# Two score tiles in one two-bank tile with one exponential, during the second MLP product of a fused attention and token-mixer kernel

## The chip, the cores and the metric

The kernel runs on one core of a Trainium2 chip. The metric is the device time of one execution in microseconds (us). A kernel is timed in several runs, and one more execution is recorded by the hardware profiler; all shares and durations below are from that one. The engines are TensorE (PE, with its weight loads as PEld), VectorE (DVE), ScalarE (ACT), GpSimd (POOL) and SyncE (SP), which issues the DMAs. Matmuls write PSUM, which has eight banks of 512 f32 columns; ACT and DVE read it from there.

## The reference

```
g = sigmoid((x * gate_w).sum(-1, keepdims=True))
# attention: 2048 tokens, 32 query heads of 20, one shared key/value head
q = (x @ wq) by head;  k = x @ wk;  v = x @ wv
p = softmax(q k^T * 20 ** -0.5)
a = (p v, heads side by side) @ wo
# token mixer: the MLP runs along the token axis, 2048 -> 1728 -> 2048, for 640 channels
u = gelu(layernorm(x)^T @ w1 + b1)
b = (u @ w2 + b2)^T
out = g * a + (1 - g) * b
```

All is f32. The MLP uses `A_x` as its input, as the attention does.

## The kernel before

**Units and stretches.** Attention is cut into 512 units: a block of 512 queries, a group of four heads (32 such pairs, `NU`), and one of 16 blocks of 128 keys. A unit has four *score* matmuls (`s`, line 684; 62 rows of the array, 512 columns), each followed by one exponential on ACT (line 695) from the PSUM bank into an SBUF buffer `p`, 128x512. A *max* matmul (`m`, line 515) computes scores the other way round, and a DVE reduction (line 521) takes their row maxima, which the scores of the next head group need. The last step of a unit is the product of its four `p` buffers with `v` (line 798), called PV here.

The middle of the program is a row of 244 *stretches* (`main`, line 1188). A stretch holds the score and max matmuls for two units and a share of the MLP or output projection, the `F` matmuls of 320 columns; it ends with PV of two units, 16 matmuls. In stretches 0 to 83 the F matmuls are the rest of the first MLP product, in 84 to 211 the second MLP product (`b2_jobs`, line 865), in 212 to 243 the output projection. Every matmul of a stretch but PV uses half the array's rows, so two *lanes* run side by side: one has the F matmuls, the other most of the scores and maxima; the halves swap from stretch to stretch.

**The order.** `ORDER` (line 1149) is a table of strings, one for each number of F matmuls in a stretch: `F` is an F matmul, `s` and `m` a score and a max on the other lane, `S` and `M` the same on the F lane. The second MLP product has stretches of 20 F (96 of them) and of 21 F (32). PE runs its instructions in program order, so a matmul that waits holds back all behind it, on both lanes.

**Banks.** `g_bank` holds the F matmuls' accumulator. The other seven banks are seven separate one-bank tiles: three named `ms`, three named `s`, one named `o`. They lie in one list (`pool`), with the time at which a small planner expects each to be free (`after`, `bank_give`); `bank_take` gives the one that is free first, to a score, a max or PV alike, so that a name says nothing of what a bank holds. The semaphore waits are not written by hand: the framework adds them, from the tiles that each instruction writes and reads.

**p buffers.** `next_p` (line 661) asks a pool of `NP` = 12 buffers for the next one.

**Tail.** The last 24 units run in blocks (`BLOCKS`) with larger groups; a block issues the scores up to one or two ahead of what its PV needs.

Of the kernel before, what the change touches and what calls it, by code (L numbers as in the profile page):

```python
# [45 lines left out]
def mix_kernel(ctx: ExitStack, tc: tile.TileContext, A_x, A_wq, A_wk, A_wv, A_wo,  # L46
# [417 lines left out]
    u0 = upool.tile([P, 2 * FC * HD2], F32R, name="u0")  # L464
    u_hi = [view(t, 0, FC) for t in (u0, slot[0])]
    u_lo = [view(t, FC * HD2, FC) for t in (u0, slot[0])]
    pp_pool = ctx.enter_context(tc.tile_pool(name="pp", bufs=NP))
    ev = ctx.enter_context(tc.tile_pool(name="ev", bufs=1))
    mpool = ctx.enter_context(tc.tile_pool(name="mpool", bufs=2))
    mmpool = ctx.enter_context(tc.tile_pool(name="mmpool", bufs=2))  # L470
# [184 lines left out]
    ptiles = {}  # L655
    spare = [False]
    sc = [0, 0]
    ring = [None] * NP
    ready = {}

    def next_p():
        ring.append(ring.pop(0))
        return pp_pool.tile([P, NB], F32, name="p") if ring[-1] is None else ring[-1]

    def s_next(b):
        j = sc[b]
# [10 lines left out]
    def qk(u, pr, b):  # L677
        n, kb = units[u]
        assert n in back_in
        if kb == 4 and pr == 0 and b == 0:  # L680
            new_q(n + 1)
        q = qtiles[n]
        s = lead_bank() if ps_l else bank_take()
        nc.tensor.matmul(s, kst[64 * b:64 * b + 62, kb * P:(kb + 1) * P], q[64 * b:64 * b + 62, pr, :],  # L684
                         start=True, stop=True)
        ready[u] = 0.0 if ps_l else max(ready.get(u, 0.0), bank_give(s, "exp"))
        if not ps_l and len(ptiles) >= len(ring):
            late.append(pool.pop()[1])
        p = next_p()
        ptiles[u, 2 * pr + b] = p  # L690

        behind, last["ins"] = last["ins"], None

        def exp():
            e = nc.scalar.activation(p, s, AF.Exp, scale=SCALE)  # L695
            if behind is not None:
                tc.add_manual_dep(e.ins, behind.ins.name, SYNC, reason="row tiles that share a bank")
                last["sig"] = e

        exp()  # L700

    ps_g = ctx.enter_context(tc.tile_pool(name="ps_g", bufs=1, space=PSUM, side="right"))
    ps_s = ctx.enter_context(tc.tile_pool(name="ps_s", bufs=3, space=PSUM, side="right"))
# [82 lines left out]
    def pv_group(us, keep=False):  # L786
        n, kb = units[us[0]]
        assert units[us[-1]][0] == n
        while late:
            pool.append((max(clock["now"], clock["act"]) + 2 * PV_US, late.pop()))  # L790
        if not otile:
            otile.append(bank_take())
        o = otile[0]
        opened = not keep or kb == 0 or us[0] == len(units) - TAIL
        ends = kb + len(us) == NS
        for i, u in enumerate(us):
            for hh in range(4):
                nc.tensor.matmul(o[32 * hh:32 * hh + 32, :], v_sb[:, kb + i, :], ptiles.pop((u, hh)),  # L798
                                 start=opened and i == 0, stop=(i == len(us) - 1) and (ends or not keep),
                                 skip_group_check=True)  # L800
        if not keep:
            begin = max(clock["act"], clock["pv"] + 0.336)
            clock["act"] = begin + 0.477
            pool.append((begin + 0.657, otile.pop()))
            if kb == 0:
                sums[0] = ev.tile([P, NB], F32, name="acc", bufs=2)
                nc.scalar.activation(sums[0], o, AF.Copy)
            else:
                part = ev.tile([P, NB], F32, name="part", bufs=2)
                nc.scalar.activation(part, o, AF.Copy)  # L810
                nc.gpsimd.tensor_add(sums[0], sums[0], part)  # L811
        if ends and n < NU - 1:
            qb, g = divmod(n, NQ)
# [48 lines left out]
            first = (None, turned, back) if keep else (sums_out, sums_in, None, inverse, inverse_in, None, scale)  # L862
            later.extend((False, f) for f in (*first, high, low))
# [273 lines left out]
    def settle(wide=False):  # L1137
# [6 lines left out]
        for f in q_parts_due[:2]:  # L1144
# [4 lines left out]
    AHEAD, ENTER, EXIT = 4, 0.108, 0.135  # L1149
    ORDER = {26: "mFFsFmFsFFsFFmFmFsFFFsFmFFmFFsFFmFFmFFmFsMFs",  # L1150
             22: "sFmFFsFFFmsFFFmFssFFmFFFssFFFmmFFFsFmM",
             20: "MsmFFsFsFsFFFFmFFsmFmFFFFmsFsFFsFFMm",
             21: "MsFsFFmmFFsFFssFFFmsFFmFFFsmFFmFFsFFm",
             15: "sMFmFsFFmFsFFsFmFFsFFmFsFFsS",
             16: "sMFmFsFFmFsFFsFmFFsFFmFsFFsSm"}

    def order(k):
        return ORDER[len(ph[k][0]) + (k - (len(ph) - 4 * NA) in SIXES)]
# [29 lines left out]
    def main(k, vs, n_max):  # L1188
# [2 lines left out]
        fs, done = list(fs), list(done)  # L1191
        known, kept = set(row_max), set(sent)
        end = 2 * ((vs[-1] if vs else -1) + 1)
        tokens = fit(order(k), "s", end + AHEAD - sc[b])
        tokens = fit(fit(tokens, "m", n_max[b]), "M", n_max[1 - b])
        tokens = "S" * (end - sc[1 - b]) + tokens
        for i, c in enumerate(tokens):
            if i == (len(tokens) + 1) // 2:
                settle()
            if c == "F":  # L1200
                gate = max(clock["sig"], clock["g"]) if len(fs) == len(ph[k][0]) else 0.0
                issue(1 - b, F_US, fs.pop(0), gate)
                clock["behind"] = clock["end"]
                while done and not fs:
                    done.pop(0)()
            else:
                h = b if c in "sm" else 1 - b
                step = (s_next if c in "sS" else ms_next)(h)
                if step:
                    issue(h, X_US, step, min(e for e, _ in pool))  # L1210
# [20 lines left out]

    ps_l.clear()
    in_lead.close()
    ps_m = ctx.enter_context(tc.tile_pool(name="ps_m", bufs=3, space=PSUM))
    ps_o = ctx.enter_context(tc.tile_pool(name="ps_o", bufs=1, space=PSUM))
    tiles = [ps_m.tile([P, NB], F32, name="ms") for _ in range(3)] + s_banks
    tiles.append(ps_o.tile([P, NB], F32, name="o"))
    pool.extend(zip(FREE_AT, tiles))
    v = 0
    clock.update(now=0.0, act=ACT_AT, dve=0.5, pv=0.0)  # L1240
# [22 lines left out]
        tail_load(NS - 4 - NA + i, late=True)  # L1263

    for j, n in enumerate(BLOCKS):
        ends = [min(2 * len(units), 2 * (v + n) + (2 if n < 3 else 1)) for _ in range(2)]
        lanes = [[], []]
        own = [(2 * len(units) - c + 32 * NU - m) * X_US for c, m in zip(sc, given)]
        while any(sc[b] < ends[b] for b in range(2)):
# [46 lines left out]
    ot = ev.tile([P, NB // 32, 32], F32, name="ot")  # L1316
    rl = ev.tile([P, NB // 32], F32, name="rl")
    on = ev.tile([P, NB], F32, name="acc", bufs=2)
    oh, ol = (pp_pool.tile([P, NB], F32, name="p").bitcast(F32R) for _ in range(2))
    half = slice(NB // 2, NB)  # L1320

    def turn(a):
# [29 lines left out]

    def close(i, d):
        st = NS - 4 + i
        at = pp_pool.tile([P, NB], F32, name="p")
# [49 lines left out]
```

## Time and profile before

| | |
|---|---|
| median of the runs, us | 1600.85 (1600.8 to 1601.18, 3 runs) |
| the profiled execution, us | 1600.86 |
| its span, first to last instruction, us | 1599.1 |
| DVE busy | 1355.6 us, 85% |
| ACT busy | 1286.0 us, 80% |
| POOL busy | 868.5 us, 54% |
| PEld busy | 1124.6 us, 70% |

A page of the profile lists the busy time of each engine, the span in 40 slices, the DMA queues, the chain of work that ended last, and the costliest groups of instructions. A row such as `L521 DVE TENSOR_REDUCE mp<-s` is line 521 of the kernel, the engine, the operation, and what it writes and reads. Matmuls overlap each other, so "busy" on PE says that some matmul was under way, not that the array was full. What follows the bar of a group is the idle time of its engine just before it and the instruction that ended the wait.

### The profile page before, as it was taken

How to read it: one execution, taken by the hardware profiler on the slowest of the kernel's cores; microseconds unless marked ns; L12 is line 12 of the kernel's file. 1: busy time of each engine (PE TensorE's matmuls, PEld its weight loads, DVE VectorE, ACT ScalarE, POOL GpSimd, SP SyncE). 2: the span in 40 equal slices, each digit the busy share in tenths (PEclk: the TensorE clock that was granted, in tenths of full speed). 3: DMA queues.
4: the chain of work that ended last, by engine and by line, in shares of the span. 5: the costliest groups of instructions: out<-in, count | busy, mean ns of one | idle time of the engine just before them, and what ended most of it. 6: DMA issues, size and time to landing. Idle time of an engine off the chain costs nothing.

```text
span 1599.1 us, 39478 instructions
## 1 busy us (share of the span) xinstructions
PE 1593.2 (100%) x14864; PEld 1124.6 (70%) x14864; DVE 1355.6 (85%) x2301; ACT 1286.0 (80%) x2566; POOL 868.5 (54%) x976
## 2 busy tenths in 40 slices
PE   9999999999999999999999999999999999999999
PEld 7899677776777667666666666666666666666676
DVE  6689999999999999988888888888888888766643
ACT  4546888888888888888888888888888888999975
POOL 6568677678778777544544344454544433344420
PEclk9999999999999999999999999999999999999999
DMA  7655223223323222222222121222222112345521
GB/s 219 213 168 147 74 66 87 75 69 95 91 79 84 80 74 73 65 73 82 74 69 67 54 68 54 82 73 82 73 74 66 59 50 67 92 122 182 169 78 59
DMA packets 183750, 145.07 MB, mean 91 GB/s; under 512 B 38291, under 2 KB 145424, under 8 KB 183560
## 3 DMA queue, kind: packets, MB, share of 16 engines
q1 hardware_dynamic: 183272, 142.23, 30.7%
q8 instruction: 117, 1.92, 0.5%
q14 instruction: 73, 0.60, 0.1%
q10 hardware_dynamic: 288, 0.33, 0.1%
HBM read 108.75 MB, written 32.15 MB: 88 GB/s over the span
## 4 chain that ended last, share of the span: by engine, by line
PE 98%; DVE 1%; issue 0%; POOL 0%; ACT 0%; DVEq 0%; POOLq 0%
PE s L798 14%; PE ms L798 12%; PE g L876 11%; PE ms L515 9%; PE s L515 8%; PE s L684 8%; PE g L1079 8%; PE ms L684 7%; PE pp L308 4%; PE o L798 4%; PE o L515 3%; PE o L684 3%; PE s L729 2%; PE g L1015 2%; PE s L970 1%; DVE mp L545 1%
## 5 line engine op out<-in xcount | busy, mean ns | idle before, releaser
L521 DVE TENSOR_REDUCE mp<-ms 128x1 f32<-128x512 f32 x909 | 596.8, 682 | 63.2 <-PE ms L515 32.6
L521 DVE TENSOR_REDUCE mp<-s 128x1 f32<-128x512 f32 x785 | 518.8, 682 | 69.6 <-PE s L515 38.4
L695 ACT ACTIVATE p<-s 128x512 f32<-128x512 f32 x915 | 535.4, 631 | 12.1 <-PE s L684 5.2
L695 ACT ACTIVATE p<-ms 128x512 f32<-128x512 f32 x796 | 473.3, 631 | 6.7 <-PE ms L684 2.8
L811 POOL TENSOR_TENSOR acc<-acc,part 128x512 f32<-128x512 f32 x213 | 275.4, 1293 | 307.2 <-ACT part L810 303.4
L684 PE MATMUL s<-qst,kst 62*128 62x512 f32 x919 | 351.4, 407 | 0.2 <-DVE yo L978 0.2
L515 PE MATMUL ms<-kst,qmx 60*128 60x512 f32 x909 | 348.8, 406 | 0.0
L684 PE MATMUL ms<-qst,kst 62*128 62x512 f32 x799 | 311.2, 409 | 0.0
L1079 PE MATMUL g<-slot,wh 64*128 64x320 f32 x1344 | 308.6, 309 | 0.0
L515 PE MATMUL s<-kst,qmx 60*128 60x512 f32 x785 | 304.3, 411 | 0.5 <-DVE mp L521 0.5
L135 POOL TENSOR_TENSOR wl<-wr,wh 128x512 fp32r<-128x512 f32 (+1 forms) x176 | 218.2, 1240 | 28.0 <-ACT wh L132 16.3
L798 PE MATMUL s<-p,v_sb 128*32 128x512 f32 x1856 | 223.2, 598 | 0.0
L1079 PEld LDWEIGHTS g<-slot,wh 64*128 64x128 f32 x1344 | 222.3, 184 | 0.0
L1079 PE MATMUL g<-slot,wl 64*128 64x320 f32 x672 | 212.3, 316 | 0.0
L515 PEld LDWEIGHTS ms<-kst,qmx 60*128 60x128 f32 x909 | 165.6, 185 | 58.2 <-ACT p L695 33.5
L798 PE MATMUL ms<-p,v_sb 128*32 128x512 f32 x1688 | 204.8, 598 | 0.0
L521 DVE TENSOR_REDUCE mp<-o 128x1 f32<-128x512 f32 x262 | 178.9, 683 | 30.5 <-PE o L515 17.4
L695 ACT ACTIVATE p<-o 128x512 f32<-128x512 f32 x308 | 194.6, 632 | 3.7 <-PE o L684 3.0
L876 PE MATMUL g<-slot,wh 64*128 64x320 f32 x864 | 195.2, 308 | 0.0
L876 PE MATMUL g<-u,wh 64*128 64x320 f32 x864 | 195.1, 308 | 0.0
L684 PEld LDWEIGHTS s<-qst,kst 62*128 62x128 f32 x919 | 169.1, 185 | 26.1 <-DVE mp L521 11.7
L515 PEld LDWEIGHTS s<-kst,qmx 60*128 60x128 f32 x785 | 142.9, 185 | 61.4 <-ACT p L695 34.6
(271 smaller groups left out, 3140.0 us busy)
## 6 DMA issues: line engine op xcount, KB each, us to landing
wr<-in_B_w_dram SPq DMA_DIRECT2D x136, 256.0 KB
qmx<-q_scr SPq DMA_DIRECT2D x192, 80.0 KB
qst<-q_scr SPq DMA_DIRECT2D x192, 80.0 KB
ot<-l_scr SPq DMA_DIRECT2D x120, 64.0 KB
y_scr<-yo SPq DMA_DIRECT2D x16, 320.0 KB
slot<-o_scr SPq DMA_DIRECT2D x16, 320.0 KB
o_scr<-ot SPq DMA_DIRECT2D x124, 40.0 KB
o_scr<-acc SPq DMA_DIRECT2D x124, 40.0 KB
```

The costliest lines, as they stand in the source:

```text
L135: nc.gpsimd.tensor_sub(wl[:, :nv], wr[:, :nv], f32(wh[:, :nv]))
L308: nc.tensor.matmul(pp, w, t, start=first and n == 0, stop=not more and n == len(steps) - 1)
L515: nc.tensor.matmul(ms, qmax[n][64 * b:64 * b + 60, pr, qt * P:(qt + 1) * P], kst[64 * b:64 * b + 60, kq * NB:(kq + 1) * NB], start=True, s ...
L521: r = nc.vector.tensor_reduce(mtiles[n][:, c, kq:kq + 1], ms, axis=AX.X, op=ALU.max)
L684: nc.tensor.matmul(s, kst[64 * b:64 * b + 62, kb * P:(kb + 1) * P], q[64 * b:64 * b + 62, pr, :], start=True, stop=True)
L695: e = nc.scalar.activation(p, s, AF.Exp, scale=SCALE)
L729: nc.tensor.matmul(pu[r][:, :HD2], w[rows, c, :], h[rows, st, :], start=(st == 0 and k == 0), stop=(st == NS - 1 and k == 2))
L798: nc.tensor.matmul(o[32 * hh:32 * hh + 32, :], v_sb[:, kb + i, :], ptiles.pop((u, hh)), start=opened and i == 0, stop=(i == len(us) - 1) a ...
L811: nc.gpsimd.tensor_add(sums[0], sums[0], part)
L876: other_tile(half, nc.tensor.matmul(hold["p"][:, :HD2], w[r, i, :], u[d][r, fc, :], start=(hold["n"] == 1), stop=(hold["n"] == 6 * FC - 3)))
L1015: other_tile(half, nc.tensor.matmul(hold["p"][:, :HD2], o[r, c, :], w[r, c, d * HD2:(d + 1) * HD2], start=(hold["n"] == 1), stop=(hold["n" ...
L1079: other_tile(half, nc.tensor.matmul(hold["p"][:, :HD2], w[r, st % HS, :], h[d][r, st, :], start=(hold["n"] == 1), stop=(hold["n"] == 6 * NS)))
```

## The change

Four of the seven banks become two tiles `ms` of two banks each. In a stretch with 20 F, two scores of one lane (`a` and `z` in the order) go to the two halves of one such tile, and a single exponential over 1024 columns reads both and writes two `p` buffers. For that, the twelve `p` buffers become slices of one tile. Outside such a pair, the four halves are handed out singly, as the banks were before; the seventh bank named `o` is gone, so the count stays at seven. The orders for 20 and 21 F are new, with the same number of matmuls of each kind. A score that finds no free `p` buffer now gets its exponential after the next PV (`deferred`). In the tail, a block no longer issues scores ahead of its own PV. Two buffers of the closing code come from other tiles.

```diff
-    pp_pool = ctx.enter_context(tc.tile_pool(name="pp", bufs=NP))
+    pp_pool = ctx.enter_context(tc.tile_pool(name="pp", bufs=1))
+    p_all = pp_pool.tile([P, NP, NB], F32, name="p")
...
-    ring = [None] * NP
+    ring = [p_all[:, i, :] for i in range(NP)]
+    p_slot = {id(p): i for i, p in enumerate(ring)}
...
     def next_p():
         ring.append(ring.pop(0))
-        return pp_pool.tile([P, NB], F32, name="p") if ring[-1] is None else ring[-1]
+        return ring[-1]
+
+    def next_pair():
+        two = sorted((next_p(), next_p()), key=lambda p: p_slot[id(p)])
+        lo, hi = (p_slot[id(p)] for p in two)
+        return two, p_all[:, lo:hi + 1:hi - lo, :]
...
+        if len(ptiles) < len(ring):
+            give()
+        else:
             late.append(pool.pop()[1])
...
+            deferred.append(give)
...
+    def pair_hold():
+        at = {id(t): e for e, t in pool}
+        whole = min(bank_pairs, key=lambda p: max(at[id(t)] for t in p[:2]))
...
+        pool[:] = [x for x in pool if x[1] is not whole[0] and x[1] is not whole[1]]
+
+    def pair_half(b):
...
+        nc.tensor.matmul(two["whole"][i], kst[64 * b:64 * b + 62, kb * P:(kb + 1) * P],
+                         qtiles[n][64 * b:64 * b + 62, pr, :], start=True, stop=True)
...
+        if pr:
...
+            pool.extend((free, two["whole"][i]) for i in two["banks"])
...
+            ps, whole = next_pair()
+            for pr, i in enumerate(two["banks"]):
+                ptiles[u, 2 * pr + b] = ps[i]
+            exp(whole, two["whole"][2], two["behind"])
...
-             20: "MsmFFsFsFsFFFFmFFsmFmFFFFmsFsFFsFFMm",
-             21: "MsFsFFmmFFsFFssFFFmsFFmFFFsmFFmFFsFFm",
+             20: "MsFsFmFFazFFmFFFsFmFFFsFmFFmFFsFsFmM",
+             21: "sFmFsFFmFFFsFFsFmsFFmFmFFFsmFFmFFsFsM",
...
-    ps_m = ctx.enter_context(tc.tile_pool(name="ps_m", bufs=3, space=PSUM))
-    ps_o = ctx.enter_context(tc.tile_pool(name="ps_o", bufs=1, space=PSUM))
-    tiles = [ps_m.tile([P, NB], F32, name="ms") for _ in range(3)] + s_banks
-    tiles.append(ps_o.tile([P, NB], F32, name="o"))
+    ps_m = ctx.enter_context(tc.tile_pool(name="ps_m", bufs=2, space=PSUM))
+    wholes = [ps_m.tile([P, 2, NB], F32, name="ms") for _ in range(2)]
+    bank_pairs = [(t[:, 0, :], t[:, 1, :], t) for t in wholes]
+    tiles = [t for p in bank_pairs for t in p[:2]]
+    tiles = tiles[:3] + s_banks + tiles[3:]
...
-        ends = [min(2 * len(units), 2 * (v + n) + (2 if n < 3 else 1)) for _ in range(2)]
+        ends = [min(2 * len(units), 2 * (v + n)) for _ in range(2)]
```

Two places of PE's order show what this does to the waits. The names carry the framework's numbers here, so that one tile can be told from another; `x2` counts equal rows that follow each other, and `[waits DVE_49]` says that the instruction waits for a count that DVE raises as its instructions end (`Activation_49` for ACT, `Pool_49` for POOL). The first place is the start of stretch 132, with 20 F matmuls, in which `s`, `ms` and `o` are banks and `g` the F accumulator. Before the change (line 515 is a max, 684 a score, 876 an F):

```order
L515 MATMUL s_1187<-kst_71,qmx_13137 128x512 [waits Activation_49]
L684 MATMUL ms_2333<-qst_13138,kst_71 128x512 [waits Activation_49]
L515 MATMUL s_1186<-kst_71,qmx_13137 128x512 [waits DVE_49]
L876 MATMUL g_1185<-u0_1163,wh_13763 128x320 [waits DVE_49,Activation_49,Pool_49]
L876 MATMUL g_1185<-u0_1163,wh_13763 128x320
L684 MATMUL ms_2331<-qst_13138,kst_71 128x512
L876 MATMUL g_1185<-u0_1163,wl_13764 128x320 [waits Pool_49]
L684 MATMUL ms_2332<-qst_13138,kst_71 128x512
```

Here the first five score and max matmuls go to five tiles. The same place after the change (line 516 is a max, 691 a score, 735 a score of the pair, 930 an F):

```order
L516 MATMUL ms_2325<-kst_71,qmx_12182 128x512 [waits Activation_49]
L691 MATMUL ms_2325<-qst_12122,kst_71 128x512 [waits DVE_49]
L930 MATMUL g_1186<-u0_1163,wh_12680 128x320 [waits Activation_49,Pool_49]
L691 MATMUL s_1188<-qst_12122,kst_71 128x512
L930 MATMUL g_1186<-u0_1163,wh_12680 128x320
L516 MATMUL s_1187<-kst_71,qmx_12182 128x512
L930 MATMUL g_1186<-u0_1163,wl_12681 128x320 [waits Pool_49]
L930 MATMUL g_1186<-u0_1163,wh_12680 128x320
L735 MATMUL ms_2326<-qst_12122,kst_71 128x512 x2
```

The first two rows write the two halves of one tile, `ms_2325`. The score in the second row goes to a half that ACT read last, and yet it waits for DVE: by the counts in the program, for the reduction of the max in the first row, which reads the other half. The framework counts readers of a PSUM tile by the whole tile, not by its banks. The second place is the end of the same stretch, up to PV (line 798 before, 849 after). Before:

```order
L684 MATMUL s_1188<-qst_13138,kst_71 128x512 [waits Activation_49]
L876 MATMUL g_1185<-u0_1163,wh_13769 128x320
L876 MATMUL g_1185<-u0_1163,wh_13941 128x320 [waits Pool_49]
L515 MATMUL ms_2333<-kst_71,qmx_13137 128x512 [waits DVE_49]
L515 MATMUL s_1187<-kst_71,qmx_13137 128x512 [waits Activation_49]
L798 MATMUL ms_2331<-p_13969,v_sb_72 32x512 [waits DVE_49]
```

The four tiles of these rows were each last written at least sixteen rows further up. After:

```order
L691 MATMUL ms_2326<-qst_12122,kst_71 128x512
L930 MATMUL g_1186<-u0_1163,wh_12686 128x320
L691 MATMUL ms_2326<-qst_12122,kst_71 128x512 [waits Activation_49]
L930 MATMUL g_1186<-u0_1163,wh_12841 128x320 [waits Pool_49]
L516 MATMUL ms_2325<-kst_71,qmx_12182 128x512 [waits DVE_49] x2
L849 MATMUL s_1188<-p_1167,v_sb_72 32x512 x8
```

The third row waits for the exponential of the score in the first row, two rows ahead. Of the two maxima in the fifth row, the second waits for the reduction of the first. From stretch 0 on, 1821 matmuls into an `ms` tile wait for a reader of the other half that comes later in the program than the last reader of their own half: 717 in stretches 1 to 83, 849 in 84 to 211, 210 in 212 to 243, 38 in the tail and 7 ahead of stretch 1.

More of the change, by code (lines that the diff above doesn't have):

```diff
@@ L686, in qk @@
         ready[u] = 0.0 if ps_l else max(ready.get(u, 0.0), bank_give(s, "exp"))
-        if not ps_l and len(ptiles) >= len(ring):
-            late.append(pool.pop()[1])
[L689 to L697, printed above, removed]
-                last["sig"] = e
@@ L700, in qk, with give, exp @@
-        exp()
+        behind, last["ins"] = last["ins"], None
+        def give():
+            assert len(ptiles) < len(ring)
+            p = ptiles[u, 2 * pr + b] = next_p()
+            exp(p, s, [behind])
+        if len(ptiles) < len(ring):
+            give()
+        else:
+            late.append(pool.pop()[1])
+            deferred.append(give)
+    deferred = []
+    def exp(p, s, behind):
+        e = nc.scalar.activation(p, s, AF.Exp, scale=SCALE)
+        for f in behind:
+            if f is not None:
+                tc.add_manual_dep(e.ins, f.ins.name, SYNC, reason="row tiles that share a bank")
+                last["sig"] = e
@@ new lines, in mix_kernel @@
+    two = {}
+    def pair_hold():
+        at = {id(t): e for e, t in pool}
+        whole = min(bank_pairs, key=lambda p: max(at[id(t)] for t in p[:2]))
+        two["banks"] = sorted(range(2), key=lambda i: at[id(whole[i])])
+        two["free"] = [at[id(whole[i])] for i in two["banks"]]
+        two["whole"], two["behind"], two["end"] = whole, [], 0.0
+        pool[:] = [x for x in pool if x[1] is not whole[0] and x[1] is not whole[1]]
+    def pair_half(b):
+        j = sc[b]
+        sc[b] += 1
+        u, pr = divmod(j, 2)
+        n, kb = units[u]
+        assert n in back_in and pr == len(two["behind"])
+        if kb == 4 and pr == 0 and b == 0:
+            new_q(n + 1)
+        i = two["banks"][pr]
+        nc.tensor.matmul(two["whole"][i], kst[64 * b:64 * b + 62, kb * P:(kb + 1) * P],
+                         qtiles[n][64 * b:64 * b + 62, pr, :], start=True, stop=True)
+        two["end"] = max(two["end"], clock["end"], clock["behind"] if last["ins"] is not None else 0.0)
+        two["behind"].append(last["ins"])
+        last["ins"] = None
+        if pr:
+            clock["end"] = two["end"]
+            free = after("act", 0.842, 0.18)
+            pool.extend((free, two["whole"][i]) for i in two["banks"])
+            ready[u] = max(ready.get(u, 0.0), free)
+            if any(f is not None for f in two["behind"]):
+                clock["sig"] = free
+            assert len(ptiles) + 2 <= len(ring)
+            ps, whole = next_pair()
+            for pr, i in enumerate(two["banks"]):
+                ptiles[u, 2 * pr + b] = ps[i]
+            exp(whole, two["whole"][2], two["behind"])
@@ L800, in pv_group @@
                                  skip_group_check=True)
+        for f in deferred:
+            f()
+        deferred.clear()
         if not keep:
@@ L1151, in mix_kernel @@
              22: "sFmFFsFFFmsFFFmFssFFmFFFssFFFmmFFFsFmM",
-             20: "MsmFFsFsFsFFFFmFFsmFmFFFFmsFsFFsFFMm",
-             21: "MsFsFFmmFFsFFssFFFmsFFmFFFsmFFmFFsFFm",
+             20: "MsFsFmFFazFFmFFFsFmFFFsFmFFmFFsFsFmM",
+             21: "sFmFsFFmFFFsFFsFmsFFmFmFFFsmFFFsFFmsM",
              15: "sMFmFsFFmFsFFsFmFFsFFmFsFFsS",
@@ L1193, in main @@
         end = 2 * ((vs[-1] if vs else -1) + 1)
-        tokens = fit(order(k), "s", end + AHEAD - sc[b])
+        tokens, need = order(k), end + AHEAD - sc[b]
+        if sc[b] % 2 or sum(tokens.count(c) for c in "saz") != need:
+            tokens = fit(tokens.replace("a", "s").replace("z", "s"), "s", need)
+        if "a" in tokens:
+            pair_hold()
         tokens = fit(fit(tokens, "m", n_max[b]), "M", n_max[1 - b])
@@ L1205, in main @@
                     done.pop(0)()
+            elif c in "az":
+                if c == "a" and not two.get("free"):
+                    pair_hold()
+                issue(b, X_US, lambda: pair_half(b), two["free"].pop(0))
             else:
@@ L1318, in mix_kernel @@
     on = ev.tile([P, NB], F32, name="acc", bufs=2)
-    oh, ol = (pp_pool.tile([P, NB], F32, name="p").bitcast(F32R) for _ in range(2))
+    o_split = qp.tile([P, 2, NB], F32R, name="qst")
+    oh, ol = (o_split[:, i, :] for i in range(2))
     half = slice(NB // 2, NB)
@@ L1354, in close @@
         st = NS - 4 + i
-        at = pp_pool.tile([P, NB], F32, name="p")
+        at = next_p()
         sl = slice(d * HD2, (d + 1) * HD2)
```

## Prediction

> **What bounds the kernel now.** I read the page first: the engines' shares, the granted clock and the chain that ended last.
>
> ```profile
> PE 1593.2 (100%) x14864; PEld 1124.6 (70%) x14864; DVE 1355.6 (85%) x2301; ACT 1286.0 (80%) x2566; POOL 868.5 (54%) x976
> ...
> PEclk9999999999999999999999999999999999999999
> ...
> PE 98%; DVE 1%; issue 0%; POOL 0%; ACT 0%; DVEq 0%; POOLq 0%
> ```
>
> The chain is PE for 98% of the span, at full clock. So time can be won only where PE stands, and every wait that is added to PE's queue is paid in full, unless PE would have stood there anyway. Second, the windows by stage:
>
> ```profile
> 163.00:652.00 489.00, 489.00 (x4740) 345.67 (x4731) 458.82 (x782) 409.25 (x812) 364.35 (x427) 1.00 0.30 80
> 652.00:1365.00 713.00, 713.00 (x6696) 487.27 (x6688) 633.78 (x1074) 594.52 (x1186) 322.05 (x349) 1.00 0.23 67
> 1365.00:1520.00 155.00, 155.00 (x1420) 97.64 (x1418) 101.70 (x171) 150.41 (x306) 65.53 (x67) 1.00 0.47 144
> 1520.00:1599.00 79.00, 75.13 (x762) 54.20 (x758) 34.56 (x66) 48.51 (x94) 8.51 (x13) 0.99 0.22 69
> ```
>
> After window and length the columns are busy us of PE, PEld, DVE, ACT, POOL, then clock, DMA share and GB/s. The rows are the first MLP product, the second, the output projection and the tail. In the second, 128 stretches take 713 us, 5.57 each; ACT is busy 594.52 of it and DVE 633.78, so neither is full. Third, the timeline of one stretch with 20 F, cut to what the terms need:
>
> ```profile
> 919.70 0.49 PE L515 MATMUL s<-kst,qmx 60*128 60x512 f32 x1
> ...
> 919.70 0.50 PE L684 MATMUL ms<-qst,kst 62*128 62x512 f32 x1
> ...
> 920.04 0.39 PE L515 MATMUL s<-kst,qmx 60*128 60x512 f32 x1
> ...
> 920.23 1.29 DVE L521 TENSOR_REDUCE mp<-s 128x1 f32<-128x512 f32 x2 [0.68 <-PE ms L684]
> ...
> 922.04 1.28 DVE L521 TENSOR_REDUCE mp<-ms 128x1 f32<-128x512 f32 x2
> ...
> 922.98 0.50 PE L515 MATMUL s<-kst,qmx 60*128 60x512 f32 x1
> ...
> 923.41 0.16 PEld L798 LDWEIGHTS ms<-p,v_sb 128*32 128x32 f32 x8 [0.25 <-DVE mp L521]
> 923.41 1.93 PE L798 MATMUL ms<-p,v_sb 128*32 128x512 f32 x16
> ...
> 925.26 0.18 PEld L515 LDWEIGHTS ms<-kst,qmx 60*128 60x128 f32 x1 [0.84 <-ACT p L695]
> ```
>
> The 36 matmuls ahead of PV take 923.41 - 919.70 = 3.71 us, **0.10 us a row** of PE's order. PV starts 0.43 us after the last of them and waits for DVE. In a stretch with 21 F it starts 0.32 us after:
>
> ```profile
> 850.73 0.39 PE L515 MATMUL ms<-kst,qmx 60*128 60x512 f32 x1
> ...
> 851.05 0.64 PE L798 MATMUL ms<-p,v_sb 128*32 128x512 f32 x4
> ```
>
> So before the change some 0.11 us stand idle ahead of PV in each of the 96 stretches with 20 F: 11 us, and little else is to be won.
>
> **The change, part by part.** *The new orders* have as many matmuls of each kind as the old, so PE's own work is the same. At best they win the 11 us above. The loss could be as much, if other places wait 0.11 us instead; I take 0 in the sum, since the next part covers every such wait, and keep both ends.
>
> *The pair's exponential.* About 96 times, one instruction over 1024 columns takes the place of two over 512.
>
> ```profile
> L521 DVE TENSOR_REDUCE mp<-s 128x1 f32<-128x512 f32 x446 | 294.2, 683 | 35.3 <-PE ms L684 18.3 <-PE s L515 6.6 <-PE s L684 5.5
> ...
> L695 ACT ACTIVATE p<-ms 128x512 f32<-128x512 f32 x448 | 265.0, 635 | 0.0
> ```
>
> The trace has none of 1024. It lies between one of 635 ns and two, 1270 ns; either way ACT gains at most 0.6 us a stretch and loses nothing. ACT is not full, so this is worth 0 on the path. *p buffers as slices*: exponential and PV wait for their own slice, as they did for their own buffer: 0. *The late exponentials* after PV, and *the closing code's other buffers*: 0, nothing new waits. *The tail's blocks* without scores ahead: each of the 7 PV blocks may now wait for its last exponential, at most one turn-round of 1.2 us (below), 0 to 8 us; I take 0, as most of a block's PV uses earlier units.
>
> *The two-bank tiles* carry the sum. Both places shown from PE's order have it: a matmul into one half of an `ms` tile waits until the reader of the other half has ended. The bank would be free; the wait is there all the same, and PE, being in order, stops on both lanes. What it costs is the turn-round from the matmul that fills the other half:
>
> - matmul start to the reduction's start, DVE idle before: 920.23 - 919.70 = 0.53. The first matmul of a stretch took 0.49 where later ones take 0.39, so 0.43 for a matmul that did not itself wait.
> - the reduction: 0.68.
> - its end to the weight load that waited for it: 922.04 + 1.28 = 923.32, load at 923.41: 0.09.
>
> That is 1.2 to 1.3 us. Over ACT it is 0.05 less, by 635 against 683 ns. I take **1.2 us** and keep 1.1 and 1.3. A wait whose feeder stands d rows ahead then stops PE for 1.2 - 0.1 d. Counted from the order, of the 1821 such waits:
>
> - 168 at one row (1.1 each), 229 at two (1.0), 121 at three (0.9): 523 us
> - 51, 119 and 148 at four, five and six rows: 41 + 83 + 89 = 213 us
> - 105, 107 and 79 at seven to nine: 53 + 43 + 24 = 119 us
> - 110 and 110 at ten and eleven: 22 + 11 = 33 us
> - 474 at twelve or more: 0
>
> Sum 888 us. Stretch 132 shows it singly: the score in its second row (one row: 1.1), a max two rows behind a score in the middle (1.0), the score in the third row of its end (1.0), the last max (1.1): 4.2 us on a stretch of 5.57. Stretch 131 has waits at 6, 7, 12, 3 and 2 rows: 0.6 + 0.5 + 0 + 0.9 + 1.0 = 3.0.
>
> Where both tiles are in use at once, a wait for the one passes partly inside a stop for the other and is not paid twice. Going down all rows in order, 0.1 us a row, and setting each waiting row to no earlier than 1.2 us after its feeder, gives 250 us in stretches 1 to 83, 427 in 84 to 211, 88 in 212 to 243 and 21 in the tail: **786 us**. With 1.1 it is 681, with 1.3 it is 899; with 1.3 and nothing shared, 1036.
>
> Sum, against the profiled execution's 1600.86 us (span 1599.1 and 1.8 around it; the median of the runs is 1600.85): 1600.9 + 786 = 2387, **2390 us**.
>
> [...]
>
> **The rivals.** *Faster: the waits find their count already reached.* Then the change does what it says: the idle time ahead of PV goes, 1600.9 - 11 = 1590 us. It decides at twelve rows between feeder and waiter, where 1.2 us have passed anyway. For it: 474 waits are that far. Against it: 518 are three rows or less. Faster 2%; no change, the 11 us being lost elsewhere, 2%.
>
> *Nothing is shared and the readers queue.* Several matmuls come at once after a stop, and a reduction stands behind another (two took 1.29 us above). Then the price is 1.3 and the sum 1036: 2640 us. For it: DVE is 89% busy in the second product. Against: in a time longer by half it has room. 12%.
>
> *The stops are shorter*, 1.1 us, and lanes that ran apart catch up during them, up to 0.3 us a stretch (a score's 0.24 and some): 1600.9 + 681 - 244 x 0.3 = 2210 us. For it: the rate of 0.1 is an average over two lanes. 10%.
>
> *The clock drops.* With PE standing a third of the time, the granted clock could fall below the 1.00 of the rows above. In the last window PE stood 79.00 - 75.13 = 3.87 us and the clock was 0.99. If half of the 1436 us from 163 to 1599 ran at half clock, 718 us would come on top: 3100 us. 3%.
>
> [...]
>
> *The change isn't what it seems*: the pair is not formed. The order has the pair's matmuls, and the waits come from the two-bank tiles with or without it, so the time would be the forecast's.
>
> **How the numbers follow.** The forecast, 2290 to 2500 us, has 71%. The range reaches from the shorter stops to the unshared ones, 2210 to 2640, and holds 93% by these cases. About 0.2% is what a measurement can tell from no change here: slower by more 96%, within 2%, faster by more 2%.
>
> **What would show it.** In the changed profile the wait view should have PEld at the max and score lines waiting for DVE and ACT, hundreds of times and hundreds of us together. Stretches should differ by their waits: some 8.6 us on average in the second product, 9.8 for those like 132 and 8.6 for those like 131. DVE and ACT should do the same work in more time, DVE 1356 of 2390, 57%. The chain should pass through DVE and ACT in a third of the span. The clock should stay at 1.00. The prediction is wrong if a score into one half starts before the reader of the other half has ended, or if the first product's stretches, whose order strings are unchanged, keep their length.

## The result and the profile after

| | before | after |
|---|---|---|
| median of the runs, us | 1600.88 (1600.77 to 1601.35, 6 runs) | 2731.81 (2721.03 to 2738.63, 6 runs) |
| the profiled execution, us | 1600.86 | 2735.35 |
| its span, us | 1599.1 | 2733.6 |

The kernel is slower: ratio 1.7063, with a 95% interval from 1.7045 to 1.708. The forecast was 2390 us, in a range of 2210 to 2640. The sign and the main cause came out as forecast; the time lies outside the range, 1131 us over before where 790 were forecast.

The page of the changed kernel has these lines where the prediction showed those of before: busy time of the engines, the granted clock in 40 slices, and the chain by engine and by line.

```profile
PE 2153.8 (79%) x14864; PEld 1206.4 (44%) x14864; DVE 1444.3 (53%) x2301; ACT 1384.3 (51%) x2470; POOL 867.0 (32%) x976
...
PEclk9998989899899988988898888988988888898899
...
PE 63%; DVE 17%; ACT 15%; issue 3%; DMA 0%; POOL 0%; ACTq 0%; SPq 0%; DVEq 0%; POOLq 0%
DVE mp L522 17%; ACT p L710 13%; PE s L849 13%; PE ms L516 12%; PE ms L849 10%; PE ms L691 8%; PE s L516 4%; PE g L930 3%; PE pp L308 3%; PE s L691 3%; PE g L1133 2%; ACT part L864 2%; PE s L780 1%; PE g L1069 1%; PE ms L1024 1%
```

Before, 98% of the chain was PE. Now 32% of it is DVE and ACT, nearly all of that the reduction (17%) and the exponential (13%), the two readers of the banks. The clock row, all nines before, is not so now; over the span the mean granted clock is 0.895. PE's busy time has grown by 561 us with the same 14864 matmuls: a matmul takes longer when the clock is halved (line 516 alone 0.79 us where it otherwise takes 0.50 after a stop), and 0.50 us instead of 0.39 after a stop, as will be seen.

The view of waits of the changed kernel gives the engine and line, what it waited for, us in total, times, and the longest:

```profile
PEld ms L516 <- DVE mp L522: 236.6, 302, 1.5
PEld ms L516 <- ACT p L710: 227.5, 254, 1.6
PEld ms L691 <- ACT p L710: 193.3, 249, 1.8
...
PEld ms L691 <- DVE mp L522: 129.4, 160, 1.5
```

Lines 516 and 691 are the max and the score, 522 and 710 the reduction and the exponential. All four rows are waits at tiles named `ms`, the two-bank ones: 965 waits and 787 us together. That this sum is near the forecast's 786 us is chance: it is idle time of the weight loads in these four rows, at either clock, not what PE lost by the stops. Before, the first row of the kind in this view was:

```profile
PEld s L515 <- ACT p L695: 34.6, 42, 0.8
```

The windows by stage of the changed kernel (length, busy us of PE, PEld, DVE, ACT, POOL, then clock, DMA share, GB/s), for first product, second product, output projection and tail:

```profile
163.00:904.00 741.00, 592.20 (x4133) 331.69 (x4137) 430.03 (x682) 384.79 (x707) 318.79 (x372) 0.91 0.17 46
904.00:2324.00 1420.00, 1083.39 (x7211) 562.87 (x7207) 736.64 (x1160) 692.25 (x1179) 361.71 (x398) 0.87 0.13 37
2324.00:2600.00 276.00, 214.13 (x1412) 108.51 (x1404) 109.17 (x175) 161.93 (x298) 63.30 (x66) 0.88 0.26 78
2600.00:2734.00 134.00, 105.17 (x879) 65.28 (x879) 43.48 (x81) 63.37 (x120) 15.15 (x19) 0.95 0.17 52
```

PE now stands for 20 to 24% of every stage, also of the first, where no order string was changed. The clock lies between 0.87 and 0.95. Since the clock records of its trace hold only full and half clock (95 of each), a mean of c over T us says that 2 x (1 - c) x T us ran at half: 2 x 0.105 x 2733.6 = **574 us** over the whole span.

One stretch shows the stops singly. Stretch 148 has the same order and the same place among eight as 132, of which the prediction spoke, and ran wholly at full clock. From its timeline: start, length, instruction, and in brackets the idle time of that engine before it and what ended it.

```profile
1681.78 0.50 PE L516 MATMUL ms<-kst,qmx 60*128 60x512 f32 x1
...
1682.31 0.69 DVE L522 TENSOR_REDUCE mp<-ms 128x1 f32<-128x512 f32 x1 [0.99 <-PE ms L516]
...
1683.06 0.50 PE L691 MATMUL ms<-qst,kst 62*128 62x512 f32 x1 [0.79 <-DVE mp L522]
...
1683.40 0.39 PE L691 MATMUL s<-qst,kst 62*128 62x512 f32 x1
...
1684.57 0.40 PE L691 MATMUL ms<-qst,kst 62*128 62x512 f32 x1
1684.59 1.51 ACT L710 ACTIVATE p<-ms 128x1024 f32<-128x1024 f32 x2
1686.15 0.18 PEld L516 LDWEIGHTS ms<-kst,qmx 60*128 60x128 f32 x1 [1.56 <-ACT p L710]
1686.15 0.50 PE L516 MATMUL ms<-kst,qmx 60*128 60x512 f32 x1 [1.19 <-ACT p L710]
...
1687.18 0.39 PE L691 MATMUL ms<-qst,kst 62*128 62x512 f32 x1
...
1688.35 0.50 PE L691 MATMUL ms<-qst,kst 62*128 62x512 f32 x1 [0.61 <-ACT p L710]
...
1688.68 0.39 PE L516 MATMUL ms<-kst,qmx 60*128 60x512 f32 x1
...
1689.85 0.18 PEld L516 LDWEIGHTS ms<-kst,qmx 60*128 60x128 f32 x1 [1.21 <-DVE mp L522]
...
1690.28 0.64 PE L849 MATMUL s<-p,v_sb 128*32 128x512 f32 x4
```

The four forecast stops are there. From the feeding matmul to the one that waits, the turn-rounds are 1683.06 - 1681.78 = 1.28, 1686.15 - 1684.57 = 1.58, 1688.35 - 1687.18 = 1.17, and 1689.85 - 1688.68 = 1.17 us, where 1.2 was taken. In the second, a single score's exponential stands behind the pair's on ACT (the row of 1.51 us is both), and that costs 0.38 more. None of the waiting matmuls starts before the reader of the other half has ended: the first reduction ends at 1682.31 + 0.69 = 1683.00, and the score starts at 1683.06. The stretch up to PV took 1690.28 - 1681.78 = 8.50 us against 3.71 before (the prediction's row): 4.79 more, where the four stops were to give 4.2. The 0.2 us that remain fit a small loss at each stop: a matmul that had to wait is 0.50 long, the others 0.39 or 0.40, and what is behind it on its lane comes some 0.10 us later.

### The profile page after: what moved, and what is told of

Same layout as the page of the kernel before. It is cut to its first block, busy times and chain, and to the rows that moved or that the text cites. A ratio compares the mean times of both kernels' runs of the same rounds, so it can differ in the third digit from the quotient of the medians.

```text
span 2733.6 us, 39922 instructions
## 1 busy us (share of the span) xinstructions
PE 2153.8 (79%) x14864; PEld 1206.4 (44%) x14864; DVE 1444.3 (53%) x2301; ACT 1384.3 (51%) x2470; POOL 867.0 (32%) x976
## 4 chain that ended last, share of the span: by engine, by line
PE 63%; DVE 17%; ACT 15%; issue 3%; DMA 0%; POOL 0%; ACTq 0%; SPq 0%; DVEq 0%; POOLq 0%
DVE mp L522 17%; ACT p L710 13%; PE s L849 13%; PE ms L516 12%; PE ms L849 10%; PE ms L691 8%; PE s L516 4%; PE g L930 3%; PE pp L308 3%; PE s L691 3%; PE g L1133 2%; ACT part L864 2%; PE s L780 1%; PE g L1069 1%; PE ms L1024 1%
## 5 line engine op out<-in xcount | busy, mean ns | idle before, releaser
L522 DVE TENSOR_REDUCE mp<-ms 128x1 f32<-128x512 f32 x1116 | 759.8, 689 | 777.6 <-PE ms L516 598.8
L710 ACT ACTIVATE p<-ms 128x512 f32<-128x512 f32 (+1 forms) x1021 | 642.9, 637 | 480.2 <-PE ms L691 350.1
L516 PE MATMUL ms<-kst,qmx 60*128 60x512 f32 x1116 | 545.0, 495 | 294.8 <-ACT p L710 142.1
L691 PE MATMUL ms<-qst,kst 62*128 62x512 f32 x932 | 427.5, 467 | 201.9 <-ACT p L710 112.1
L516 PEld LDWEIGHTS ms<-kst,qmx 60*128 60x128 f32 x1116 | 216.2, 195 | 580.4 <-DVE mp L522 236.6
L849 PE MATMUL s<-p,v_sb 128*32 128x512 f32 x2192 | 358.3, 785 | 0.0
L1133 PE MATMUL g<-slot,wh 64*128 64x320 f32 x1344 | 358.2, 339 | 0.0
L691 PEld LDWEIGHTS ms<-qst,kst 62*128 62x128 f32 x932 | 177.3, 193 | 379.2 <-ACT p L710 193.3
L849 PE MATMUL ms<-p,v_sb 128*32 128x512 f32 x1880 | 287.7, 735 | 63.0 <-DVE mp L522 53.4
L930 PE MATMUL g<-slot,wh 64*128 64x320 f32 x864 | 240.5, 342 | 0.0
L864 ACT ACTIVATE part<-s 128x512 f32<-128x512 f32 x110 | 65.7, 597 | 278.2 <-PE s L849 214.4
```

Of the source, the lines that this page charges most:

```text
L516: nc.tensor.matmul(ms, qmax[n][64 * b:64 * b + 60, pr, qt * P:(qt + 1) * P], kst[64 * b:64 * b + 60, kq * NB:(kq + 1) * NB], start=True, s ...
L522: r = nc.vector.tensor_reduce(mtiles[n][:, c, kq:kq + 1], ms, axis=AX.X, op=ALU.max)
L930: other_tile(half, nc.tensor.matmul(hold["p"][:, :HD2], w[r, i, :], u[d][r, fc, :], start=(hold["n"] == 1), stop=(hold["n"] == 6 * FC - 3)))
L1133: other_tile(half, nc.tensor.matmul(hold["p"][:, :HD2], w[r, st % HS, :], h[d][r, st, :], start=(hold["n"] == 1), stop=(hold["n"] == 6 * NS)))
```

## Experiments

The first question was which part of the change carries the loss, the second why it was larger than forecast. Each run is compared with the kernel before on the same chip (1600.96 us for e1 to e4, 1600.83 for e5 to e8).

### e1_banks: everything but the two-bank tiles

```diff
-             20: "MsFsFmFFazFFmFFFsFmFFFsFmFFmFFsFsFmM",
+             20: "MsFsFmFFssFFmFFFsFmFFFsFmFFmFFsFsFmM",
...
-    ps_m = ctx.enter_context(tc.tile_pool(name="ps_m", bufs=2, space=PSUM))
-    wholes = [ps_m.tile([P, 2, NB], F32, name="ms") for _ in range(2)]
-    bank_pairs = [(t[:, 0, :], t[:, 1, :], t) for t in wholes]
-    tiles = [t for p in bank_pairs for t in p[:2]]
+    ps_m = ctx.enter_context(tc.tile_pool(name="ps_m", bufs=4, space=PSUM))
+    tiles = [ps_m.tile([P, NB], F32, name="ms") for _ in range(4)]
```

> The changed kernel with its four banks as four one-bank tiles again, and the pair's two scores with an exponential each; new orders, p slices, late exponentials and tail as changed. If the waits across the halves of the two-bank tiles are the whole loss: 1590 to 1605 us, granted clock 1.00. If the new orders, the p slices or the tail cost part of the 1131 us: over 1650 us.

Measured: 1603.29 us, ratio 1.0014 (1.0005 to 1.0024). The four banks are separate tiles, the pair is two scores with an exponential each, and all else is as in the changed kernel. The windows of the first and the second product:

```profile
163.00:652.00 489.00, 489.00 (x4746) 345.27 (x4740) 459.87 (x783) 409.90 (x813) 365.79 (x430) 1.00 0.30 80
652.00:1365.00 713.00, 713.00 (x6664) 485.81 (x6661) 628.03 (x1069) 591.55 (x1181) 320.06 (x346) 1.00 0.23 67
```

PE doesn't stand any more, and the clock is back at 1.00. Orders, slices, late exponentials and the tail's blocks together are worth 2.3 us; the two-bank tiles with the pair carry the other 1128.5.

### e2_tiles: only the two-bank tiles

```diff
-    ps_m = ctx.enter_context(tc.tile_pool(name="ps_m", bufs=3, space=PSUM))
-    ps_o = ctx.enter_context(tc.tile_pool(name="ps_o", bufs=1, space=PSUM))
-    tiles = [ps_m.tile([P, NB], F32, name="ms") for _ in range(3)] + s_banks
-    tiles.append(ps_o.tile([P, NB], F32, name="o"))
+    ps_m = ctx.enter_context(tc.tile_pool(name="ps_m", bufs=2, space=PSUM))
+    wholes = [ps_m.tile([P, 2, NB], F32, name="ms") for _ in range(2)]
+    tiles = [t[:, i, :] for t in wholes for i in range(2)]
+    tiles = tiles[:3] + s_banks + tiles[3:]
```

> The kernel before with one edit: the seven banks are two two-bank tiles and three one-bank tiles, handed out singly; no pair, old orders, old p buffers. If the tiles alone make the loss: 2500 to 2800 us, with half-clock stretches of hundreds of us. If the pair or the new orders are needed for it: under 1800 us.

Measured: 2796.3 us, ratio 1.7466 (1.7431 to 1.7501). This is the kernel before with its old orders, no pair, and the same seven banks; only four of them are halves of two tiles. That alone costs more than the whole change. The view of cores and the page's clock row:

```profile
core 0: 2793.8 us, clock 0.876
...
PEclk9998999989998888976888877877889889888899
```

So the cause is not the exponential over two banks and not the orders: it is that the program guards each half against the reader of the other. The clock is lower still here than in the changed kernel, by the same reckoning 693 us at half.

### e3_fill and e8_half_fill: the same waits, with PE busy during them

In front of a row that has to wait, matmuls with weights of zero are put on the F lane, so many that they take 1.2 - 0.1 d us (d rows since the feeder), 3968 in all. They add nothing to the accumulator.

```diff
+    zpool = ctx.enter_context(tc.tile_pool(name="zpool", bufs=1))
+    zero = zpool.tile([P, P], F32R, name="zero")
+    nc.gpsimd.memset(f32(zero), 0.0)
...
+        d = row[0] + 1 - used.get(id(other), -99)
+        if other is not None and inside:
+            for _ in range(max(0, round((1.2 - 0.1 * d) / F_US))):
+                r = slice(64 * h, 64 * h + 64)
+                other_tile(h, nc.tensor.matmul(g_bank[:, :HD2], zero[r, :], kst[r, :HD2], start=False, stop=False))
```

In e8_half_fill the count per wait is halved, `round(0.5 * (1.2 - 0.1 * d) / F_US)`, which gives 1983.

> The changed kernel with 3968 more matmuls of 320 columns with zero weights, put on the F lane ahead of the matmuls that would wait for the other half, as many as fill the wait (some 583 us of PE work at 0.147 us each); the sums they add to are unchanged. If idle PE lowers the clock and that is part of the loss: half-clock time falls from 576 us to under 300, and the kernel is faster in spite of the added work, 2450 to 2620 us. If the stops are only longer than I priced them and the clock costs nothing: 2730 us or more.

> The kernel of e3_fill with half as many zero matmuls at the same places, 1983 in place of 3968. If the clock follows PE's share of busy time: half-clock time between the 576 us of the changed kernel and the 50 us of e3_fill, and a time between 2576 and 2732 us. If e3 was faster for another reason than the clock: no faster than 2732 us, or as fast as e3 with the clock still low.

Measured: e3_fill 2576.11 us, ratio 1.6091 (1.6059 to 1.6123); e8_half_fill 2590.08 us, ratio 1.618 (1.6133 to 1.6228). The views of cores of the two, and a line of the first:

```profile
core 0: 2570.3 us, clock 0.991
```

```profile
core 0: 2579.8 us, clock 0.974
```

```profile
L1245 PE MATMUL g<-kst,zero 64*128 64x320 f32 x3968 | 727.0, 304 | 0.0
```

With 3968 matmuls **more**, the kernel is 156 us **faster** than the changed one; with half as many it is 142 us faster. The stops are still there, and so is the longer matmul after each: at full clock, 1135 scores and maxima into an `ms` tile take 0.50 us in the trace of the changed kernel, 1262 in e8_half_fill and 1318 in e3_fill. So what these matmuls can win is the clock: at half ran 574 us in the changed kernel, 2 x 0.026 x 2579.8 = 134 in e8_half_fill and 46 in e3_fill. Between the profiled executions of the changed kernel and of e8_half_fill (2735.35 and 2581.76 us) this is 154 us for 440 us less at half, **0.35 us for each**. At this price the 574 us cost 200. The fillers of e8_half_fill may cost some time of their own, so the price is rather a lower bound; the two executions of e8_half_fill, which differ by 16.6 us and in clock (0.974 and 0.966, some 41 us at half), give 0.40. From e8_half_fill to e3_fill the clock rises again and the time hardly falls, so the last fillers do begin to cost time of their own.

### e4_pair_only and e5_six: a two-bank tile without false waits

One tile of two banks is kept for the pair. Its second half takes part in pairs only, its first half is also handed out singly, so that readers of different halves meet only where a pair begins; the other banks are single. Six banks are then left for all else, one fewer than before.

```diff
-        whole = min(bank_pairs, key=lambda p: max(at[id(t)] for t in p[:2]))
+        whole = bank_pairs[0]
+        at[id(whole[1])] = two.get("other", 0.0)
...
-            pool.extend((free, two["whole"][i]) for i in two["banks"])
+            pool.append((free, two["whole"][0]))
+            two["other"] = free
...
+    whole = ps_w.tile([P, 2, NB], F32, name="w")
+    bank_pairs = [(whole[:, 0, :], whole[:, 1, :], whole)]
+    tiles = [ps_m.tile([P, NB], F32, name="ms") for _ in range(2)] + [bank_pairs[0][0]] + s_banks
```

> The changed kernel with one two-bank tile, whose second half is used by pairs alone; the other banks are one-bank tiles, six for single use in place of seven. The pair and its exponential over 1024 columns stay. If the loss is the waits across halves: 1595 to 1680 us, clock 1.00, the rest being the missing bank. If the long exponential or the pair itself holds PE: over 1800 us. The trace gives the time of the long exponential, which I put between 0.635 and 1.27 us.

Measured: 1734.98 us, ratio 1.0837 (1.0819 to 1.0856), above the 1595 to 1680 us expected. The granted clock is 1.00. What was missed is not the pair: the stretches of the first product, which have none, are longer by 39.9 us in all, 0.48 each, and those of the second by 55.8, 0.44 each. The seventh bank is missing everywhere but in the pairs. e5_six takes the pair out of this kernel and leaves the six banks:

```diff
-             20: "MsFsFmFFazFFmFFFsFmFFFsFmFFmFFsFsFmM",
+             20: "MsFsFmFFssFFmFFFsFmFFFsFmFFmFFsFsFmM",
```

> The kernel of e4_pair_only (1735 us) without the pair: its two scores go to single banks with an exponential each; six banks for single use, new orders otherwise. If e4's loss is the missing seventh bank, which all stretches miss: within 10 us of 1735. If the pair and its exponential of 1047 ns cost e4 time: under 1715 us. If the pair wins ScalarE time that matters: over 1755 us.

Measured: 1747.2 us, ratio 1.0917 (1.0902 to 1.0932). This is 12 us above e4_pair_only, a little outside the 10 us expected if the missing bank is the whole loss. Six banks instead of seven cost 1747.2 - 1603.3 = 144 us. Of this, 31 us lie in the tail, where the second half of `w` is handed out as well, so that some of them may be waits across the halves. The first product is longer than before by 39.8 us, as in e4_pair_only. In the second product, the only place that has pairs, e4_pair_only is 6.3 us shorter than e5_six; most of the other 6 us lie in the tail, which has none. So the pair *wins* about 6 us where banks are short, and as its second half is a seventh bank that only the pair uses, no run shows whether the single exponential has any part in it. The price of its exponential, by shape in the changed kernel and then in e4_pair_only:

```profile
L710 ACT ACTIVATE p<-ms 128x1024 f32<-128x1024 f32 x96 | 98.5, 1026 | 26.3 <-PE ms L735 23.4
```

```profile
L710 ACT ACTIVATE p<-w 128x1024 f32<-128x1024 f32 x96 | 100.5, 1047 | 0.2
```

It lies between the bounds of 635 and 1270 ns that the prediction set.

### e6_old_orders: e1 with the orders of before

```diff
-             20: "MsFsFmFFssFFmFFFsFmFFFsFmFFmFFsFsFmM",
-             21: "sFmFsFFmFFFsFFsFmsFFmFmFFFsmFFFsFFmsM",
+             20: "MsmFFsFsFsFFFFmFFsmFmFFFFmsFsFFsFFMm",
+             21: "MsFsFFmmFFsFFssFFFmsFFmFFFsmFFmFFsFFm",
```

> The kernel of e1_banks (one-bank tiles, no pair, 1603.3 us) with the old orders for 20 and 21 F matmuls; left of the change are the p slices, the late exponentials and the tail. If the new orders made e1's 3.7 us in the second MLP product: 1598 to 1601 us. If the p slices or the late exponentials did: 1603 again.

Measured: 1600.64 us, ratio 0.9999 (0.999 to 1.0008). The slices, the late exponentials, the closing buffers and the tail's blocks cost nothing together. The new orders without their pair are 2.6 us behind the old ones: every run of e1_banks took longer than every run of e6_old_orders, though the two intervals still touch. (The string for 21 F that the changed kernel ran with is the one in this diff; the diff ahead of the prediction shows its last letters otherwise.)

### e7_aware: the changed kernel, with a planner that knows of the wait

When a half is given back, its partner's expected time is raised to the same value, so that the planner no longer hands out a half whose partner is being read.

```diff
+    def give_back(free, bank):
+        pool.append((free, bank))
+        for p in bank_pairs:
+            for t, o in (p[:2], p[1::-1]):
+                if t is bank:
+                    pool[:] = [(max(x, free), y) if y is o else (x, y) for x, y in pool]
```

> The changed kernel with the two-bank tiles, pairs and orders, but the planner now counts a half as taken as long as the other half is, so that it hands out other banks first. By the order, waits with a feeder under twelve rows ahead fall from 1347 to 352 and those at three rows or less from 518 to 8; walked as in the prediction 92 us are left of 786, and 0.1 us of restart for each of 370 stops. If the count of short waits sets the loss: 1700 to 1850 us, the rest being banks that are held longer, and the clock over 0.98. If the loss has another source in the change: over 2300 us.

Measured: 1842.42 us, ratio 1.151 (1.1489 to 1.1531), as expected. Counted from the program's order, the waits with fewer than twelve rows between feeder and waiter fall from 1347 to 352, and those with three or fewer from 518 to 8. The page's clock row and chain:

```profile
PEclk9999999999999999999999999999999999999999
...
PE 80%; DVE 11%; ACT 6%; issue 1%; DMA 1%; POOL 1%; SPq 0%; ACTq 0%; DVEq 0%; POOLq 0%
```

So 889 of the 1131 us go by choosing among the same tiles in another order, and the clock stays up. What is left, 242 us, is in part the remaining waits and in part that two banks are now often held for one reader; how it divides was not measured.

No version beat both kernels: e6_old_orders equals the kernel before within 0.1%. What might, a pair that reads two banks which the program guards one by one, was not tried.

## Why the prediction was right in kind and too small

**What bounds the kernel: right.** PE had no room (98% of the chain), so each wait added to its queue was paid.

**The small parts, 0 in the sum: right.** Late exponentials, slices, closing buffers and tail are worth 0 (e6_old_orders), the orders 2.6 us on the side of loss, inside the 11 us either way. The pair's exponential took 1026 ns, between the two bounds; what it is worth on the path with seven banks and no waits across halves, no run shows.

**The two-bank tiles as the cause: right.** e1_banks takes them out and the loss is gone; e2_tiles has them alone and loses 1195 us. In e1_banks the same four banks have a tile each, so that the program guards none against the reader of another, and the kernel takes 1603.29 us. The program's waits decided, not the banks.

**The price of a stop: mis-sized.** The turn-round of 1.2 us was right where one reader stood free (1.28, 1.17 and 1.17 in stretch 148). Two things were left out of the stops' term of 786. A matmul that waited takes 0.50 instead of 0.39 and sets back its lane by some 0.10; the prediction saw this in its own rows ("the first matmul of a stretch took 0.49 where later ones take 0.39") and counted it for the first row of a stretch only. Going down the rows as the prediction did, 1163 waits stop PE, which by this reckoning makes 116 us. And the pair's exponential holds up a second reader, 0.38 us in stretch 148.

What the stops cost at full clock can be read from the trace. Stretches with the same place among eight and the same stops agree within 0.1 us when they run wholly at full clock, and for 189 of the stretches 1 to 243 one of the same kind did. At its length, these 189 would be 657 us longer than in e1_banks, where the prediction's way down the rows gives 585: 12% more. (For single stretches it is wrong by up to 1.3 us, in either direction, so it is right as a sum rather than row by row.) On 786 this makes 883. From the other side, the profiled 2735 us less 200 to 235 for the clock (below) are 900 to 935 over before. So the term is **880 to 935 us, not 786**. By itself this would have left the time inside the range.

**The clock: this step failed.** The sum took 1.00 throughout, and the rival "the clock drops" had 3%; both were the author's estimate, as the profile of before, with PE busy 1593.2 of its 1599.1 us, could not show what many short stops do to the clock. The runs showed a clock that halves with no long stop ahead. Windows of the changed kernel, from the stretch before 140 on; the first number after the length is PE's busy time:

```profile
1596.87:1601.87 5.00, 3.69 (x28) 1.57 (x30) 2.31 (x4) 2.31 (x5) 2.91 (x3) 1.00 0.30 102
1601.87:1606.87 5.00, 3.19 (x31) 2.48 (x27) 3.27 (x5) 3.56 (x6) 1.45 (x2) 1.00 0.51 149
1606.87:1613.69 6.82, 6.04 (x25) 1.70 (x22) 1.77 (x3) 1.49 (x3) 0.28 (x1) 0.50 0.13 44
1613.69:1618.69 5.00, 3.13 (x29) 2.50 (x27) 2.80 (x5) 2.79 (x5) 0.98 (x1) 1.00 0.00 0
```

PE was busy for 74% and then 64% of 5 us at full clock, with no stop over 1.2 us, and then the clock was halved for 6.82 us. The clock records of the whole trace have 95 such drops, and in the 5 us ahead of one no stop is longer than 1.5 us (the last, at the program's end, aside). In these 5 us PE was busy 64% in the median, nine times in ten at most 70%. The rest of the time at full clock from 163 us on, taken in 266 whole pieces of 5 us, has a median of 80%, and nine in ten of them have at least 64%. The fillers test it as a cause: they leave the waits and give PE more to do, 91% of the span in e3_fill, and the clock returns to 0.991.

The busy share is not itself what decides, though: in e8_half_fill PE was busy 72% in the median shortly ahead of its drops, where the changed kernel, taken the same way, had 57%, and 70 of those 266 pieces at full clock had less than 72%. What does decide, no run shows.

What a drop costs is seen in stretches 140 and 148, with the same order and the same stops:

```profile
1599.92:1612.47 12.55, 9.17 (x56) 4.22 (x53) 5.34 (x8) 4.89 (x8) 2.52 (x2) 0.78 0.39 124
1681.78:1692.13 10.35, 6.98 (x56) 3.94 (x52) 5.34 (x8) 4.90 (x8) 2.52 (x2) 1.00 0.60 169
```

The first is 2.20 us longer, with 2 x 0.22 x 12.55 = 5.5 us at half clock: 0.40 us for each. The end of its timeline, at half clock:

```profile
1608.18 0.79 PE L516 MATMUL ms<-kst,qmx 60*128 60x512 f32 x1 [0.78 <-DVE mp L522]
1608.90 3.64 PE L849 MATMUL s<-p,v_sb 128*32 128x512 f32 x16
1612.47 0.79 PE L516 MATMUL s<-kst,qmx 60*128 60x512 f32 x1
```

Most of the 2.20 is PV, all PE's own work: 1612.47 - 1608.90 = 3.57 us against 1692.13 - 1690.28 = 1.85, which is 1.72 of the 2.20. Against those of the same kind at full clock, the 189 stretches above lost 122 us in 298 at half, 0.41 for each. By 0.35 to 0.41, the 574 us cost **200 to 235 us**. So the loss of 1131 is 786 as forecast, 95 to 150 more for the stops, and 200 to 235 for the clock. Neither alone would have left the range: 2387 with 150 more is 2537, and with 235 more 2622. It took both, and the clock is the larger and the one that the sum put at nothing. The rival's price for it, 718 us, was three times too much.

**The signs.** Stretches like 132 were to take 9.8 us and took 10.35 at full clock; most of them ran partly at half, so that they took 12.1 on average. Stretch 131 was to take 8.6 and took 8.9 with a part at half. The second product's stretches were to take 8.6 on average and took 10.4, with both of the missing terms in it. DVE was to be busy 57% and was 53%. The chain was to be DVE and ACT for a third: 32%. The first product's stretches lengthened with their order strings unchanged. Hundreds of waits at the max and the score came as said, and no waiting matmul of stretch 148 started before the reader of the other half had ended. The clock was to stay at 1.00 and was 0.895.

## What to carry to other kernels

Before several tiles are merged for one wide instruction, look at who else uses the parts: a framework that guards by tile makes independent users of one tile wait for each other, and on an engine that runs in order each such wait costs the whole turn-round through the other engine (1.2 us here), less what lies between. If a change puts many short stops on PE, put a lower clock in the forecast even when no stop is long (at most 1.5 us ahead of the drops here, the last aside), and price it (here 574 us at half, with 0.35 to 0.41 us lost for each). When the tile must stay, tell the planner what the program will wait for: that alone won back 889 of 1131 us.

## What the runs showed of the hardware that was not expected

- The granted clock can halve without any long stop: 95 drops in the changed kernel, with stops of at most 1.5 us in the 5 us before (the last drop aside). PE's busy share alone does not tell them (57% in the median shortly ahead of a drop in the changed kernel, 72% in e8_half_fill).
- Matmuls that compute nothing can pay: 3968 of them made the kernel 156 us faster, by the clock (0.991 instead of 0.895), with the stops and the longer matmuls after them still there.
- A matmul that had to wait takes 0.50 us where one in a running row takes 0.39 or 0.40, at full clock in both cases.
- One PSUM bank of seven is worth some 110 to 144 us to this kernel, 7 to 9% (the tail's 31 us left out or counted), though PE was busy for 1593 of 1599 us before.
